# Issuing the value loads of an attention + token-mixer kernel on Scalar's DMA queue instead of Sync's

## Chip, cores, metric

One core of one Trainium2 chip. The metric is the device time of one execution in microseconds (us), the median of several runs. "Fast" runs alone are compared; a run is called slow when it is over 1.5% above the fastest of the same kernel. PE is the matmul engine, PEld its weight load, DVE Vector, ACT Scalar, POOL GpSimd, SP Sync. ACTq and SPq are the instruction sequencers of ACT and SP, which also issue the DMAs (140 of 141 on SP, one on ACT in the trace of before).

## The reference

Eight batches, each with 8 heads, 576 positions and 64 channels: local attention (a band of 7 keys) plus attention over groups of four positions, then a token mixer with w_q, w_k and w_out.

```python
q_d, k_d, v_d = (mean of 4 neighbours of q, k, v)            # 144 positions
out_up    = np.repeat(sm_attn(q_d, k_d, v_d), 4, axis=2)
mask      = np.abs(pos[:, None] - pos[None, :]) < 4
out_local = softmax(where(mask, scale * q @ k.T, -1e9)) @ v
x = (out_up + out_local)                                      # (8, 576, 512)
W = (x @ w_q) @ (x @ w_k).T / sqrt(64)
return np.maximum(W @ x, 0) @ w_out                           # 8 x 576 x 512, float32
```

## The kernel before

In this kernel every DMA is issued by one engine, in its program order (Sync's timeline shows the ten v loads of a batch one behind the other, 10.27 us). The value loads are ten per batch, one for each half of five windows: 64 partitions x 8 heads x 64 channels, 128 KB in pieces of 256 bytes.

```python
def load_qk(b):      # q and k 1 MB each, then the remainders r (two loads of 128 KB), all on sp
    ...
def load_v(b):
    v32 = st[b]["v32"] = big.tile([128, NW, H, D], FP32, name="v32", tag="v32")
    for n in range(NW):                       # NW = 5
        for c in range(2):
            sp.dma_start(v32[64 * c:64 * c + 64, n],
                         _ap(v[b], K0[2 * n + c] * D, [[D, 64], [S * D, H], [1, D]]))
...
load_qk(0); load_v(0)                         # then w_q, w_k, load_qk(1), w_out; load_v(1) falls
...                                           #   between "tq" and "tk" of batch 0 (order below)
ORDER = [                                     # one period; (lag, step)
    (-2, "og1"), (-1, "wtd"), (0, "sums"), (1, "cast_qk"), (-1, "wt"), (0, "vd"), (0, "mask0"),
    (0, "score0"), (-1, "wks"), (2, "load_qk"), (1, "cast_v"), ...
    (0, "cs0"), (-1, "mx1"), (0, "cs1"), (0, "av4"), (0, "weights"), (-1, "mxr"), (1, "tq"), (0, "ca0"),
    (2, "load_v"), (-1, "og0"), (0, "ca1"), (1, "tk"), (1, "tr"), (-1, "ol"), (0, "xt0"), (0, "xt1"),
    (0, "odt"),
]
```

What matters of ACT's work: `tq` and `tk` end in its copies qT and kT (PSUM to SBUF), `og0` and `og1` in its copies os, `odt` in odT. `load_v(2)` stands in the order right behind qT and ahead of the first os. Other names in the profiles: PE writes the PSUM tiles pq and pk (transposes of q and k, copied to qT and kT), psc and pav (scores, and their product with v), pcs (scores of the groups), px and pod (transposes, copied to xT and odT), pwd (which needs odT) and po (the output, copied to os). E and Ec are the exponentials of the scores; kd and kdt are sums of four keys.

The softmax here doesn't subtract the row's maximum and nothing guards it: scores larger than these inputs give would overflow.

Of the kernel before, what the change touches and what calls it, by code (L numbers as in the profile page):

```python
# [13 lines left out]
def _ap(t, off, dims):  # L14

    return bass.AP(t.tensor, t.offset + off, dims)
# [14 lines left out]
def kernel(  # L31
# [12 lines left out]
    sp = _InOrder(tc, nc.sync)  # L44
    pool = _InOrder(tc, nc.gpsimd)
    act = _InOrder(tc, nc.scalar)
# [54 lines left out]
    def load_v(b):  # L101
        v32 = st[b]["v32"] = big.tile([128, NW, H, D], FP32, name="v32", tag="v32")
        for n in range(NW):
            for c in range(2):
                sp.dma_start(v32[64 * c:64 * c + 64, n],
                                  _ap(v[b], K0[2 * n + c] * D, [[D, 64], [S * D, H], [1, D]]))

    st = [{} for _ in range(B)]
    load_qk(0)
    load_v(0)  # L110
    wqk16 = cst.tile([128, 4, 2 * DH], FP16, name="wqk16")
    wo16 = cst.tile([128, 4, DM], FP16, name="wo16")
# [488 lines left out]
    for b in range(B):  # L601
        d_ = {"load_qk": (lambda b=b: load_qk(b)), "load_v": (lambda b=b: load_v(b)),
              "weights": weights if b == 0 else (lambda: None)}
        for stage in (stage_cast, stage_a, stage_b, stage_c):
            d_.update(stage(b))
        steps.append(d_)
# [36 lines left out]
```

## Time and profile before

| | before |
|---|---|
| median of 3 runs | 193.03 us (192.62 to 193.21) |
| steady period per batch | 19.30 us |
| kT of batch 0 starts | 16.32 us |
| vblk of batch 0 (first tile that gates the attention) | 27.20 us |

From the page of the kernel before: busy time by engine, the DMA queues (packets, MB, share of 16 engines), and the chain that ended last, by engine.

```profile
PE 155.5 (81%) x2720; PEld 104.0 (54%) x2720; DVE 114.8 (60%) x286; ACT 110.7 (57%) x140; POOL 107.7 (56%) x122
...
q1 hardware_dynamic: 73920, 40.12, 81.7%
...
PE 68%; DVE 17%; ACT 7%; issue 4%; POOL 2%; ACTq 0%; DVEq 0%
```

PE is the longest in the sum and carries two thirds of the chain. Nearly all data goes through one queue, q1, which is Sync's.

### The profile page before, as it was taken

The numbers are of one execution on the slowest core, as the hardware profiler recorded it, in microseconds if no ns is written. First come the engines' busy times: TensorE is split into PE (matmuls) and PEld (weight loads), VectorE is DVE, ScalarE is ACT, GpSimd is POOL, SyncE is SP. The second block draws the span as 40 slices with busy tenths as digits, with TensorE's granted clock in tenths as the row PEclk, the third lists the DMA queues.
The fourth block names the chain that finished last, engine by engine and source line by source line (L and its number), as shares of the span: only waits on it lengthen the run. The fifth ranks groups of instructions, "written<-read, shape, count | busy, mean of one in ns | idle before, by whom it ended". The sixth has DMA issues, their size and how long they took to land.

```text
span 192.7 us, 6374 instructions
## 1 busy us (share of the span) xinstructions
PE 155.5 (81%) x2720; PEld 104.0 (54%) x2720; DVE 114.8 (60%) x286; ACT 110.7 (57%) x140; POOL 107.7 (56%) x122
## 2 busy tenths in 40 slices
PE   0034448885899989998999899989998999898790
PEld 0034227853576647664776476647764776465330
DVE  6263978754646566656665666566656665685220
ACT  2037134954565767576757675767576757633422
POOL 5701991099748991895479547954895476000000
PEclk9999555999789999999999999999999999999997
DMA  5999999899899799967999899969996943004215
GB/s 175 314 187 215 348 290 162 191 354 175 175 319 218 174 264 294 263 137 201 278 323 156 184 280 346 187 154 296 330 215 154 300 146 112 3 3 153 93 57 188
DMA packets 74027, 40.54 MB, mean 210 GB/s; under 512 B 52432, under 2 KB 68880, under 8 KB 74000
## 3 DMA queue, kind: packets, MB, share of 16 engines
q1 hardware_dynamic: 73920, 40.12, 81.7%
q8 instruction: 21, 0.34, 0.7%
q14 instruction: 6, 0.05, 0.1%
q10 hardware_dynamic: 80, 0.03, 0.1%
HBM read 30.67 MB, written 9.44 MB: 208 GB/s over the span
## 4 chain that ended last, share of the span: by engine, by line
PE 68%; DVE 17%; ACT 7%; issue 4%; POOL 2%; ACTq 0%; DVEq 0%
PE po L27 15%; PE psc L27 6%; PE pav L27 5%; PE pw L27 4%; PE px L27 4%; PE pca L27 4%; PE pol L27 4%; DVE kd_127 L27 3%; PE pv L27 2%; PE pcs L27 2%; ACT kT L27 2%; PE pod L27 2%; DVE rz L27 1%; PE pws L27 1%; PE pwd L27 1%
## 5 line engine op out<-in xcount | busy, mean ns | idle before, releaser
L27 ACT COPY os<-po 128x1024 f32<-128x1024 f32 x16 | 16.2, 1012 | 14.7 <-issue 8.3
L27 DVE RECIPROCAL rz<-pav 128x8 f32<-128x8 f32 x40 | 8.1, 204 | 13.4 <-PE pav L27 13.4
L27 PE MATMUL po<-wo_91,rmx_227 128*128 128x512 f16 x64 | 15.3, 379 | 0.6 <-ACT rmx_227 L27 0.6
L27 PE MATMUL po<-wo_91,rmx_212 128*128 128x512 f16 x64 | 15.1, 379 | 0.0
L27 DVE COPY xT<-px 128x928 f16<-128x928 f16 (+1 forms) x32 | 13.8, 451 | 0.6
L27 PE MATMUL pq_236<-id_67,q_229 128*128 128x128 f16 x16 | 1.9, 312 | 12.6 <-DVE q_229 L27 12.6
L27 PE MATMUL psc<-id_67,neg 64*128 64x232 f16 (+1 forms) x80 | 9.4, 278 | 2.8 <-DVE vblk_201 L27 2.8
L27 PEld LDWEIGHTS <-rmx_227 128*128 128x128 f16 x80 | 7.2, 98 | 8.1 <-ACT rmx_227 L27 0.7
L27 PE MATMUL psc<-qT,kT 64*64 64x58 f16 (+1 forms) x640 | 11.4, 198 | 0.0
L27 PEld LDWEIGHTS <-rmx_212 128*128 128x128 f16 x80 | 7.2, 98 | 6.6
L27 DVE RECIPROCAL rc<-pca 128x8 f32<-128x8 f32 (+1 forms) x16 | 3.4, 211 | 11.8 <-PE pca L27 11.8
L27 PEld LDWEIGHTS <-wqk_90 128*128 128x128 f16 x96 | 8.3, 98 | 3.7 <-issue 0.9
L27 PEld LDWEIGHTS <-kT 64*64 64x64 f16 x640 | 8.7, 113 | 2.1 <-issue 2.1
L27 ACT COPY odT<-pod 128x448 f16<-128x448 f16 (+1 forms) x16 | 5.6, 402 | 6.3 <-PE pod L27 6.3
L27 PE MATMUL pw<-xT,wqk_90 128*128 128x288 f16 x64 | 9.2, 286 | 0.0
L27 PEld LDWEIGHTS <-q_229 128*128 128x128 f16 x16 | 1.6, 146 | 12.6 <-DVE q_229 L27 12.6
L27 POOL CAST v_0_147<-v_79 128x2560 f16<-128x2560 f32 x1 | 3.1, 3129 | 9.3 <-DMA w_92<-in_moe_w_k_dram 9.3
L27 DVE TENSOR_TENSOR wT_219<-pw,wTd 128x576 f16<-128x576 f32 x4 | 3.0, 758 | 8.6 <-ACT wTd L27 8.6
L27 DVE COPY ol<-pol 64x512 f32<-64x512 f32 x8 | 5.5, 682 | 4.3 <-PE pol L27 4.3
L27 DVE TENSOR_TENSOR wT_204<-pw,wTd 128x576 f16<-128x576 f32 x4 | 3.0, 758 | 8.0 <-ACT wTd L27 6.6
L27 DVE TENSOR_SCALAR rmx_227<-pmx 128x1024 f16<-128x1024 f32 x4 | 4.9, 1224 | 4.1 <-PE pmx L27 4.1
L27 POOL CAST v_1_149<-v_255 128x2560 f16<-128x2560 f32 x1 | 2.3, 2323 | 8.6 <-DMA v_255<-in_v_dram 8.6
(542 smaller groups left out, 540.9 us busy)
## 6 DMA issues: line engine op xcount, KB each, us to landing
out_dram<-os SPq DMA_DIRECT2D x16, 512.0 KB, 4.4
v_79<-in_v_dram SPq DMA_DIRECT2D x10, 128.0 KB, 4.6
v_255<-in_v_dram SPq DMA_DIRECT2D x10, 128.0 KB, 5.4
v_583<-in_v_dram SPq DMA_DIRECT2D x10, 128.0 KB, 3.5
v_1024<-in_v_dram SPq DMA_DIRECT2D x10, 128.0 KB, 4.4
v_1497<-in_v_dram SPq DMA_DIRECT2D x10, 128.0 KB, 3.6
v_1970<-in_v_dram SPq DMA_DIRECT2D x10, 128.0 KB, 4.3
v_2443<-in_v_dram SPq DMA_DIRECT2D x10, 128.0 KB, 3.4
```

The costliest lines, as they stand in the source:

```text
L27: return lambda *a, **k: self._tc.keep_in_program_order(f_(*a, **k))
```

## The change

The intent: Sync issues almost without a pause, Scalar is busy 57% of the time, so let Scalar's queue take the loads of v.

```diff
         for n in range(NW):
             for c in range(2):
-                sp.dma_start(v32[64 * c:64 * c + 64, n],
+                act.dma_start(v32[64 * c:64 * c + 64, n],
                                   _ap(v[b], K0[2 * n + c] * D, [[D, 64], [S * D, H], [1, D]]))
```

## The prediction

> **What bounds the kernel now.** I read the page's busy shares first, then three periods of the steady loop as windows, then the Sync and Scalar engines' own timelines, and last the chain of work that ended last. The windows each run from one copy of kT to the next:
>
> ```profile
> core 0: us, PE busy (x) PEld busy (x) DVE busy (x) ACT busy (x) POOL busy (x), PEclk, DMA share, GB/s
> 96.59:115.90 19.31, 18.53 (x344) 12.44 (x342) 12.33 (x30) 13.23 (x18) 13.59 (x12) 1.00 0.93 235
> 135.19:154.49 19.30, 18.52 (x344) 12.43 (x342) 12.31 (x30) 13.22 (x17) 13.59 (x12) 1.00 0.91 246
> ```
>
> PE is busy 18.5 of 19.3 us in each batch's period: the steady loop is PE's. DMA is at 0.93, so close behind, and ACT has 6.1 us of room. Who issues what is in the timeline of the Sync engine's queue (start, duration, tile), one period of it:
>
> ```profile
> 91.00 0.46 SPq L27 DMA_DIRECT2D q_1710<-in_q_dram  x1
> 91.56 1.80 SPq L27 DMA_DIRECT2D k_1711<-in_k_dram  x1
> 93.44 3.63 SPq L27 DMA_DIRECT2D r_1712<-in_q_dram  x1
> 97.13 1.40 SPq L27 DMA_DIRECT2D r_1712<-in_k_dram  x1
> 98.62 10.27 SPq L27 DMA_DIRECT2D v_1970<-in_v_dram  x10
> 108.99 1.13 SPq L27 DMA_DIRECT2D out_dram<-os  x1
> 110.21 0.51 SPq L27 DMA_DIRECT2D out_dram<-ol  x1
> 110.81 0.72 SPq L27 DMA_DIRECT2D out_dram<-os  x1
> ```
>
> Sync issues without a pause for about 20 of each 20 us, half of it for the ten v loads. That looks like a bound, but the period stays 19.30 us in the stretch where the last loads run out, so Sync is just keeping up and nobody waits for it in the loop. One v load by itself (tile view; min/median/max in ns):
>
> ```profile
> L27 SPq DMA_DIRECT2D v_1497<-in_v_dram x10: 633/976/2201, 77.0 to 88.2; - x10
> ```
>
> The minimum, 633 ns (with 45 ns to the next: 0.68 us), is the bare issue; the larger values come at the head of a block, right behind q and k (2 MB). Now the place in Scalar's work where the block will go, between qT and the first os:
>
> ```profile
> 111.33 0.38 ACT L27 ACTIVATE rmx_227<-pmr 128x256 f16<-128x256 f32 x1 [0.18 <-PE pmr L27]
> 112.34 1.86 ACT L27 COPY qT<-pq_2408 128x2048 f16<-128x2048 f16 x1 [0.63 <-PE pq_2408 L27]
> 114.53 1.01 ACT L27 COPY os<-po 128x1024 f32<-128x1024 f32 x1 [0.32 <-PE po L27]
> 115.90 1.86 ACT L27 COPY kT<-pk_2480 128x2048 f16<-128x2048 f16 x1 [0.36 <-PE pk_2480 L27]
> 118.49 0.70 ACT L27 COPY odT<-pod 128x448 f16<-128x448 f16 x2 [0.73 <-PE pod L27]
> 120.26 1.01 ACT L27 COPY os<-po 128x1024 f32<-128x1024 f32 x1 [1.07 <-issue]
> ```
>
> Between qT's end (114.21) and os there are 0.3 us, not ten issues' worth. In the start-up the chain runs through the very copy that the second block of loads will stand in front of:
>
> ```profile
> 14.55 1.86 ACT qT L27
> 16.42 1.78 ACT kT L27
> 18.22 1.37 DVE sum_296 L27
> 19.61 5.71 DVE kd_127 L27 x4
> 25.32 1.88 DVE kdt_129 L27
> 27.20 0.68 DVE vblk_201 L27 x2
> 27.93 0.37 PE psc L27 x2
> ```
>
> [...]a v load holds Sync 0.63 us and lands 3.6 us after its start (median). [...]a wait record of ACT starts at 112.37, while qT (112.34 to 114.21) is still copying. But another wait record stands directly ahead of qT, at 112.29: it waits for PE's transposes, and the sequencer passes it only when qT can start. [...]the trace has such a window (clock 0.5 from 50.6 to 54.0) after PE's idle gap of 46.2 to 48.5.
>
> **The change part by part.** Nothing is removed or added; PE, DVE and POOL keep their instruction order. Eighty DMA issues leave Sync for Scalar, as eight blocks of ten, each in one piece: v of batch 0 ahead of everything on ACT, v of batch 1 between qT and kT of batch 0, the others after qT of the next batch. Each DMA also waits for one of eight completion counters, that is, for the landing of an earlier DMA, now across both queues.
>
> *Five loop blocks (batches 3 to 7), exposed.* Measure from e, the end of the second os copy (101.97 in the period shown, 121.28 the next: 19.3).
> - Until qT nothing changes: 112.34 - 101.97 = e+10.4.
> - The block starts there (the wait ahead of qT). Sync is now free at e, so q, k and the r pair are issued at once. By the page's packets they need about 8.9 us of the engines with os and 2 us of latency, about e+11.5; the block's waits for their landing (fifth load on) are met. So 10 x 0.68 = 6.8 us: end at e+17.2.
> - os 1.0 (e+18.3), kT 1.86 (e+20.1). PE had run on through ca, po, pk, pol to e+15, then stands: px needs the PSUM tile that os empties, and the next po the one that kT empties. po 1.73: e+21.9, second os 1.0: e+23.0.
> - Period 23.0 against 19.3: +3.7, less than the 4.8 us that os comes later, as odT and its wait overlap kT. Five periods: +18.5.
>
> *Half clock.* PE stands some 3.4 us per period. That may drop its clock in a following window, as it did after the 2.3 us gap. A window at half clock costs up to 1.7; I take 0.8 on average: +4 for five.
>
> *The block of batch 2.* Its qT has one wait only, with no wait record ahead of it, so the sequencer can issue the block while the copies ahead of it still stand in the queue (E4, Ec0, Ec1, two weight casts, qT: several us of waits). Hidden: 0.
>
> *Start-up, two blocks.* The first block competes with q and k[...], and neg, the table load and the cast of k stand behind it in order. The last v load waits for the second r, neg for the w_q load, which waits for a landing too. Estimate from packet times (1 KB 46 ns, 256 B 18 ns, on 16 engines) and 2 us latency: k lands about 11.5 (before 9.8), neg leaves at 14.3, k's cast ends at 18 (before 11.8). The second block waits in turn for q, r and wo of batch 1 and k of batch 2: first load at 19.5, k of batch 2 lands about 32.7, block done at 34, so kT starts at about 34.4 instead of 16.4: +18. The chain shown (DVE sums, vblk, psc) follows whole. It is my least certain term (+10 to +24).
>
> *Sum:* 193 + 18.5 + 4 + 18 = 233; the start-up's PE work is at half clock already and a part of my landing estimates is pessimistic, so I take 230.
>
> **The rivals.**
> - *Room on ACT hides it (same time).* 13.2 busy plus 6.8 of issue is 20.0, less 1.9 that lies under qT: 18.1 of 19.3. By sum it fits. Against it: ACT's room is scattered in gaps of 0.2 to 1.2 us, and the block is in one piece at a place with 0.3.[...]
> - *Two queues are faster (faster by some per cent).* Sync is full, DMA at 0.93, outputs leave 12 us after os is copied (75.9 to 88.9). Against: the loop is PE's at 18.5 of 19.3, and the start-up chain waits for q and k, which now share the DMA engines with v. At best v of batch 0 comes earlier, and the 5 us of PE wait for it at 16.7 to 21.8 go: 188. I hold this unlikely.
> - *Back-pressure makes the block longer.* If ACT's issues are held as Sync's first v loads are (1.2 to 2.2 us, 10 to 11.8 a block), a period becomes 26 to 27: +35 to 40 in the loop, 245 to 255. Against: in the new order q and k have drained when the block starts.
>
> **Range and chances.** Loop +12 (partly hidden) to +30 (back-pressure, half clock), start-up +10 to +24: 214 to 247 holds it 8 times in 10. Slower by over 2% 0.96, within 2% 0.03, faster 0.01.
>
> **What would show it.** Right: the v blocks on ACTq start with qT and take about 6.8 us each; os follows each block at once, with ACT idle for about 5 us before it; period near 23 us from batch 3's block on, and back to 19.3 after the last; PE waits at px for os; kT of batch 0 starts near 34; DMA share falls below 0.85. Wrong: blocks that start well ahead of qT (sequencer runs ahead), blocks of 10 us (back-pressure), kT of batch 0 before 25, or a period under 20.5.

Parts of the recorded texts, here and below, are cut (each cut is marked). No term of the sum is cut: 193 + 18.5 + 4 + 18 was put as 233 and taken as 230. Gone are the argument that moving issues wins no bandwidth, and a depth to which Scalar's sequencer can run ahead, with the 205 to 215 us of the first rival that rested on it. What stays is shown in the trace of the kernel before as follows:

- Completion counters: the 141 DMAs use eight semaphores. In all 101 cases in which the trace has the landing of the DMA that had the semaphore last, the next one on it starts after that landing.
- Packet times: medians of 46 ns for 1 KB and 18 ns for 256 B. The "2 us latency": the shortest time from issue to landing is 2.28 us (ol, 128 KB), of which 64 packets of 2 KB at 86 ns on 16 engines are some 0.34.
- Half clock: the granted clock was 0.5 for 3.41 us (50.62 to 54.03), and half of that is the 1.7 of the text. The average of 0.8 is the author's guess.
- A sequencer ahead of its engine: by one wait record (112.37, within qT's 112.34 to 114.21). That it gets ahead of the copies named in batch 2 was the author's guess.
- That the first block competes with q and k: shown only afterwards, by k of batch 0, which landed at 12.46 us with the block in place and at 9.85 before.

## The result, and the profile after

The changed kernel takes **236.36 us** (median of 4 runs, 234.43 to 238.32) against 192.94 (4 runs, one more than in the table above, 192.62 to 193.21): slower, ratio 1.222, 95% interval 1.2141 to 1.2298. Here and below a ratio is the mean time of one kernel's fast runs over that of the other's of the same rounds, so not quite the ratio of the medians quoted. The profiled run is a fast one with a span of 235.7 us, against 192.7 before: 43.0 us more.

The same lines of the page as above, of the changed kernel:

```profile
PE 160.6 (68%) x2720; PEld 105.1 (45%) x2720; DVE 109.1 (46%) x286; ACT 109.3 (46%) x140; POOL 106.8 (45%) x122
...
q1 hardware_dynamic: 31680, 29.63, 44.4%
...
q10 hardware_dynamic: 42320, 10.52, 22.0%
...
PE 45%; DMA 20%; ACT 12%; DVE 9%; ACTq 7%; issue 5%; SPq 0%; DVEq 0%
```

The busy times hardly change, so no work was added. The chain did: DMA, ACT and ACT's sequencer now carry 39% of it. (Issuing is not counted as busy, so ACT's 46% hides the blocks of loads.)

**The loop.** Two periods of the changed kernel as windows, from one second os to the next (length, then busy time and count of PE, PEld, DVE, ACT and POOL, clock, DMA share, GB/s):

```profile
90.57:113.49 22.92, 19.07 (x340) 12.37 (x340) 12.41 (x29) 12.96 (x19) 13.58 (x13) 1.00 0.79 213
113.49:135.92 22.43, 19.03 (x340) 12.43 (x340) 12.40 (x29) 12.94 (x18) 13.58 (x13) 1.00 0.80 218
```

22.4 to 22.9 us instead of 19.3, with PE standing for 3.4 to 3.9 us (length less PE's busy time) and the DMA engines less loaded (0.79 against 0.93). Scalar's own timeline shows the cause (start, duration, instruction; in brackets how long ACT idled and who ended it):

```profile
103.33 1.87 ACT L27 COPY qT<-pq 128x2048 f16<-128x2048 f16 x1 [0.87 <-PE pq L27]
103.41 6.79 ACTq L27 DMA_DIRECT2D v<-in_v_dram  x10
110.24 1.01 ACT L27 COPY os<-po 128x1024 f32<-128x1024 f32 x1 [5.04 <-PE px L27]
```

The block begins 0.08 us after qT and holds the sequencer for 6.79 us; os follows 0.04 us after it. PE's po, which os empties, was finished at 105.43 (103.54 + 1.89). The bracket names PE's px because its semaphore was the last the profile saw; the sequencer was in fact at the loads. In the kernel before, the same os stood 0.3 us after qT.

**The start-up.** ACT's timeline of the first two blocks, and behind it the chain of waits of the changed kernel:

```profile
0.80 15.02 ACTq L27 DMA_DIRECT2D v<-in_v_dram  x10
...
22.02 22.00 ACTq L27 DMA_DIRECT2D v<-in_v_dram  x10
44.06 1.87 ACT L27 COPY kT<-pk 128x2048 f16<-128x2048 f16 x1 [20.72 <-DMA v<-in_v_dram]
```

```profile
1.31 11.15 DMA k<-in_k_dram
12.48 5.18 DMA v<-in_v_dram
...
18.33 10.09 DMA r<-in_k_dram
28.49 14.22 DMA k<-in_k_dram
...
44.06 1.88 ACT kT L27
...
47.36 0.85 DVE kd L27 x4
```

The second block takes 22 us where ten bare issues take 6.8. Six of its loads start 0.02 to 0.03 us after the landing of an earlier DMA: three of Sync's, and three v loads of Scalar's own. Four of the six:

| load of the second block starts | a landing just before |
|---|---|
| 22.02 | q of batch 1, 22.00 |
| 27.01 | last v of batch 0 (Scalar's own), 26.98 |
| 30.70 | w_out (first half), 30.68 |
| 42.73 | k of batch 2, 42.71 |

The kernel has eight completion counters for its DMAs: in the trace its 141 DMAs use eight semaphores, 17 or 18 each. Each of the 133 DMAs that follow another on its semaphore starts after that one's landing, 20 of them 0.02 to 0.05 us after it (on either queue, behind landings of either queue). So here a DMA that takes a counter waits until the DMA that took it last, eight places earlier in the order in which they are handed out, has landed, whichever engine issued it. That is not the order of the source: k of batch 2 comes in it ahead of the ninth v load of batch 1. On Sync alone the wait was nearly free: in the kernel before, each v load of a block starts 0.04 to 0.05 us after the end of the issue ahead of it, and none of the 101 DMAs for which that trace has the landing on their counter starts within 0.06 us of it. Split over two queues, Scalar at batch 0 waits for k of batch 2.

**Where the 43.0 us came from.** From the times of the same instructions in both traces:

| | before | after | added |
|---|---|---|---|
| start-up: vblk of batch 0 | 27.20 | 48.39 | +21.2 |
| block of batch 2: kT of batch 1 | 37.05 | 62.91 | +25.9, so +4.7 more |
| block of batch 3: second os of that period | 62.37 | 90.57 | +28.2, so +2.3 more |
| four more blocks: periods of 22.92, 22.43, 23.70, 22.50 | 19.30 each | | +14.4 |
| the last periods | | | +0.4 |

In the start-up kT comes 27.7 us later, but some 6.5 us are given back: the four DVE sums kd took 5.71 us before and 0.85 now, and kdt 1.88 and 0.18. POOL was at work beside them before and is idle now. In the trace of before three of the four sums end 0.14 us after the POOL instruction beside them (21.89 after 21.75, 23.99 after 23.85, 25.32 after 25.18); the fourth, which started just ahead of its POOL instruction, took 0.27. That POOL's work held them is the author's reading of these times: no experiment moved it away. The third row mixes causes: before has a PE gap and half clock between 46.19 and 54.0 in it, after has half clock from 63.7 to 70.5. The period of 23.70 also holds a PE gap of 1.18 us of the kind that experiments 9 to 11 are about.

### The profile page after: what moved, and what is told of

It is laid out like the page before. It is cut to its first block, busy times and chain, and to the rows that moved or that the text cites. A ratio compares the mean times of both kernels' runs of the same rounds, so it can differ in the third digit from the quotient of the medians.

```text
span 235.7 us, 6369 instructions
## 1 busy us (share of the span) xinstructions
PE 160.6 (68%) x2720; PEld 105.1 (45%) x2720; DVE 109.1 (46%) x286; ACT 109.3 (46%) x140; POOL 106.8 (45%) x122
## 4 chain that ended last, share of the span: by engine, by line
PE 45%; DMA 20%; ACT 12%; DVE 9%; ACTq 7%; issue 5%; SPq 0%; DVEq 0%
DMA k<-in_k_dram 11%; ACTq L27 7%; PE po L27 7%; PE pm L27 6%; DMA v<-in_v_dram 5%; ACT kT L27 5%; PE psc L27 5%; DMA r<-in_k_dram 4%; DVE x L27 4%; PE pav L27 4%; PE pw L27 4%; ACT Ec L27 3%; PE pq L27 3%; PE pcs L27 2%; PE pol L27 2%
## 5 line engine op out<-in xcount | busy, mean ns | idle before, releaser
L27 POOL TENSOR_TENSOR sum<-qT 128x1152 f32<-128x1152 f16 x8 | 16.9, 2107 | 45.0 <-DVE qT L27 45.0
L27 POOL CAST v<-v 128x2560 f16<-128x2560 f32 x8 | 18.6, 2326 | 33.8 <-DMA r<-in_q_dram 17.7
L27 PE MATMUL po<-wo,rmx 128*128 128x512 f16 x128 | 30.5, 380 | 3.6 <-DVE xT L27 3.0
L27 DVE TENSOR_TENSOR x<-pav,rz 128x512 f16<-128x512 f32 x40 | 27.7, 692 | 1.4
L27 ACT COPY kT<-pk 128x2048 f16<-128x2048 f16 x8 | 15.0, 1870 | 26.1 <-DMA v<-in_v_dram 25.8
L27 PEld LDWEIGHTS <-rmx 128*128 128x128 f16 x160 | 14.2, 98 | 18.5 <-DVE xT L27 3.8
L27 POOL TENSOR_TENSOR sum<-kT 128x1152 f32<-128x1152 f16 x7 | 14.8, 2107 | 15.3 <-ACT kT L27 15.3
L27 ACT ACTIVATE E<-psc 128x928 f16<-128x928 f32 (+1 forms) x24 | 19.5, 812 | 3.7 <-PE psc L27 2.7
L27 PE MATMUL pav<-v,E 64*64 64x65 f16 x640 | 18.3, 199 | 3.8 <-issue 1.2
L27 PEld LDWEIGHTS <-E 64*64 64x64 f16 x640 | 14.9, 113 | 11.9 <-issue 8.6
L27 PE MATMUL pq<-id,q 128*128 128x128 f16 x128 | 10.1, 242 | 12.9 <-DVE q L27 12.7
L27 ACT COPY qT<-pq 128x2048 f16<-128x2048 f16 x8 | 14.9, 1865 | 4.3 <-PE pq L27 4.3
```

The costliest lines, as they stand in the source:

```text
L27: return lambda *a, **k: self._tc.keep_in_program_order(f_(*a, **k))
```

## The experiments

All twelve kernels were correct.

### 1. The loop's blocks alone

```diff
-                act.dma_start(v32[...
+                (act if b >= 2 else sp).dma_start(v32[...
```

> The loads of values of batches 0 and 1 are back on Sync; batches 2 to 7 stay on Scalar in their blocks of ten. Theory (a block holds Scalar between qT and the copy after it): start-up as before (kT of batch 0 at 16.3 us), about +3.6 us in each of five loop periods and +5 us for batch 2: 193 + 22 = 215 us, 211 to 219. Rival (nearly all of the loss is the start-up, the loop only has a slightly longer period through shared DMA engines): at most 203 us.

Measured: 227.38 us (225.53 to 229.18) against 193.96, ratio 1.1674 (1.1584 to 1.1764). More than the 211 to 219 expected, so a miss, and more than the loop's share in the whole change. The start-up is that of before (kT at 16.31). The block of batch 2 took 1.37 + 10.16 us: its fifth to ninth load each start 0.02 us after the landing of the block's own load four places earlier (37.18 after 37.16, for example), as Sync's DMAs had taken the other four counters, and those own loads took 3.0 to 6.5 us to land. So kT of batch 1 came 8.7 us later. The following periods were 24.7, 22.8, 27.0 and 22.8 us. The blocks in them (6.8 to 7.9 us) are those of the whole change; the two longer ones also hold a stretch of half clock, behind a 1.67 us wait of PE for Ec in the first and behind a PE gap of 2.99 us with no releaser, only "issue", in the second. So the blocks explain about 22.8 a period, and something else the rest: experiments 9 to 11.

### 2. The first block alone

```diff
+                (act if b == 0 else sp).dma_start(v32[...
```

> Only the ten loads of batch 0 on Scalar. Theory (the block stands ahead of neg, the table load and the cast of k): k's cast starts about 10 us later than before (9.9), kT about 7 us later (near 23), part of which comes back as the DVE sums no longer run beside POOL: 196 to 201 us. Rival (the first block is free because Scalar waits for k anyway, the second block is the whole start-up loss): 192 to 194 us.

Measured: 201.86 us median of 199.24, 204.49, 198.57 and 204.91, two of them slow runs, so no interval; the fast two, 198.57 and 199.24, are some 5 us above before and agree with the expectation (profiled span 197.2). kT of batch 0 starts at 22.96 (16.32 before), as the cast of k stands behind the ten issues in ACT's order, and vblk at 32.19.

### 3. The second block alone

```diff
+                (act if b == 1 else sp).dma_start(v32[...
```

> Only the ten loads of batch 1 on Scalar, between qT and kT of batch 0. Theory (the block waits for landings of Sync's q, k, r and wo loads through the shared counters, beyond its bare 6.8 us): the block takes 12 to 22 us, kT of batch 0 starts at 27 to 37 instead of 16.3, and the time is 200 to 212 us. Rival (only the bare issue counts): block 6.8 us, kT at about 22, 193 to 198 us.

Measured: 195.99 us, ratio 1.0099 (1.0041 to 1.0157): below the range, a miss. The block took 10.85 us and kT came 9.1 us later, but vblk only 4.1 us later:

```profile
28.74 2.42 DVE L27 TENSOR_TENSOR kd<-sum 128x116 f16<-128x116 f32 x4
```

2.42 us for the four sums where before has 5.71. Of a delay ahead of those sums a part is returned by them. Of the 4.1 us some 2 more were made up later, as the median is 2.0 above that of before. The trace has no PE gap by "issue" (experiments 9 to 11) and from 38.1 us on no half clock, where before has both; whether this made them up was not tested. All four waits of the block, once begun, were for its own earlier loads, not for Sync's q, k, r and w_out as the expectation had it.

### 4. All of v in the start-up (batches 0 and 1)

```diff
+                (act if b < 2 else sp).dma_start(v32[...
```

> Batches 0 and 1 on Scalar, batches 2 to 7 on Sync: the start-up of the changed kernel alone. Theory (the two blocks feed each other: the first holds back Sync's loads of batch 1 through the counters, and the second waits for exactly those): kT of batch 0 near 44 us and vblk near 48 us as in the changed kernel, 193 + 21 = 214 us, 210 to 218, although the blocks alone cost about 6 and 2. Rival (the two just add up): 199 to 204 us.

Measured: 213.98 us, ratio 1.0976 (1.091 to 1.1043): as expected. The second block takes 21.38 us and kT of batch 0 starts at 42.66. One block costs 5 us (fast runs), the other 2, both 20: the second waits for landings that come later with the first in place (k of batch 2 at 40.63; the load that waits for it starts at 40.65). The costs of the parts do not add up, and the waits for landings, of both queues, are why.

### 5. The loads spread over ACT's period

Batches 0 and 1 on Sync; the ten loads of the others on ACT, one or two at a time behind E0, E1, E4, mx0, qT, os and kT.

```diff
-        (0, "score0"), (-1, "wks"), ...
+        (0, "score0"), (2, "lv0"), (-1, "wks"), ...        # lv0 .. lv9: one load each, on act
```

> Batches 0 and 1 on Sync; the ten loads of batches 2 to 7 stay on Scalar, but one or two at a time behind long copies (E, rmx, qT, os, kT), where the sequencer issues while the engine copies. Theory (the place of the block is what costs, not the queue): the period goes back to 19.3 to 20.0 us and the time to 192 to 197 us. Rival (Scalar's issue time or the sharing of DMA engines between two queues costs by itself, wherever it stands): 6.8 us more of Scalar's time per batch, 205 to 217 us.

Measured: 221.73 us (215.74 to 225.43, three of the four runs slow): a clear miss. A load by itself still takes 0.60 at best, but others last up to 1.92, and others again start only behind a landing of q, k or r, in whose flight they are issued (a load at 107.92 behind q's landing at 107.90; one at 114.31 behind k's at 114.29). The profiled run has a mean clock of 0.873.

### 6. The same, only where q, k and r have landed

Loads behind qT (2), os (1), kT (2), odT (1), the second os (1), E0 (1), E1 (2); POOL's cast of v moved behind the last of them.

> As the first spread version, but the ten loads stand where q, k and r of the period have already landed: two behind qT, one behind os, two behind kT, one behind odT, and in the next period one behind the second os and three behind the E copies. Theory (the first spread version failed because its loads waited on Scalar for landings of q, k and r through the shared counters, and PE's clock fell for it): no load waits more than 0.3 us, the period is 19.3 to 20.3 us and the time 193 to 201 us. Rival (loads on Scalar cost their issue time wherever they stand, or sharing the DMA engines slows the loop): 208 us and more.

Measured: 210.57 us, ratio 1.0828 (1.0748 to 1.0909). The expectation failed as a time, but one of its periods came out as hoped. Windows of this run, from second os to second os:

```profile
93.04:112.93 19.89, 18.77 (x344) 12.39 (x341) 12.33 (x29) 13.20 (x17) 11.47 (x11) 1.00 1.00 248
112.93:136.03 23.10, 20.10 (x344) 12.93 (x342) 12.42 (x29) 13.30 (x18) 15.67 (x15) 0.93 0.83 213
```

19.89 us holds all ten issues on ACT with only 0.6 us lost: there is room for them in pieces. The next period has a PE gap of 2.44 us by "issue" and a clock of 0.93.

### 7. Twenty half loads a block

```diff
+                for h2 in range(2):                        # 32 partitions each, batches 2 to 7
+                    act.dma_start(v32[64 * c + 32 * h2:64 * c + 32 * h2 + 32, n], ...
```

> As the version with only the loop's blocks on Scalar (227 us), but each load is cut in two of 32 partitions, so 20 issues of half the descriptors per block. Theory[...]: an issue takes near 0.35 us, a block stays at 7 to 8.5 us and the time at 222 to 236 us. Rival (a fixed cost per issue): 0.65 us each, a block of 13 us and more, six blocks of 6 us: 255 us and more.

Measured: 261.69 us, ratio 1.3471. ACT's timeline, the block of one period:

```profile
105.19 10.99 ACTq L27 DMA_DIRECT2D v<-in_v_dram  x20
```

The same bytes, but 10.99 us instead of 6.79. A half load holds the sequencer 0.46 us with 0.50 from one to the next, a whole one 0.65 with 0.69. By these two points an issue costs about 0.31 us (estimated: 2 x 0.50 - 0.69) plus 0.38 for its 512 pieces. The block's length sets the time in this direction: with twenty issues the period of this block is 27.9 us (from 91.56 to 119.47, at a clock of 0.93, so part of it is half clock). The block of batch 2 took 23.61 us, with landings in its way again.

### 8. The start-up's sums in one instruction (kernel before otherwise)

```diff
+                if b == 0:
+                    add(kd.rearrange(...)[:, :, :, 0:29], s_[..., 0], s_[..., 1], op=ALU.add)   # all 4 pairs
```

> The kernel before with one change elsewhere: the four sums kd of batch 0 on DVE are one instruction. In the kernel before each of these small DVE instructions ends only when a POOL instruction beside it ends (5.7 us for four), in the changed kernel, with POOL idle, the four take 0.85 us. Theory (each DVE instruction waits out one POOL instruction, so fewer instructions wait less): kd and kdt end 3 to 5 us earlier and the time is 188 to 191 us. Rival (the slowdown goes by the amount of work, or the chain has another end): 192 to 194 us.

Measured: 193.77 us against 194.01, ratio 1.0004 (0.9939 to 1.0068): no gain. (Of the four sums of before, it is three that end with a POOL instruction, 0.14 us after it.) The sum took 2.64 us in one piece, the four 5.71 before, and vblk came 2.9 us earlier (24.26), so the sums' own delay shrank as thought, but the time was lost again further on; the trace shows two PE gaps by "issue" (30.10 to 31.21 and 45.90 to 47.29) that were open at that point.

### 9 to 11. What is the PE gap by "issue"?

Every such gap of a microsecond or more, in all these runs (12 in the runs without filler), stands at 193 or 194 of PE's instructions modulo 256; in the two looked at closest (before and experiment 1) it is in the middle of a row of equal matmuls of one tile. The trace's PE instructions, counted in order of start, and the packets of the DMA queue named "instruction" (21 of 16 KB in the kernel before); five of the gaps:

| kernel | PE stands | ahead of PE instruction no. | modulo 256 | last packet | PE goes on after the packet's end |
|---|---|---|---|---|---|
| before | 46.19 to 48.52 | 961 | 193 | 45.64 to 46.99 | 1.53 |
| after | 142.76 to 143.93 | 3010 | 194 | 141.57 to 142.56 | 1.37 |
| experiment 1 | 129.34 to 132.34 | 3010 | 194 | 129.90 to 130.84 | 1.50 |
| experiment 6 | 77.95 to 79.89 | 1729 | 193 | 77.43 to 78.60 | 1.29 |
| experiment 6 | 119.30 to 121.74 | 3010 | 194 | 119.27 to 120.26 | 1.48 |

The gaps stand whole multiples of 256 instructions apart (give or take one), and 21 packets against 5440 PE instructions (2720 matmuls, 2720 weight loads) make 259 to a packet. The author's reading is that these packets bring PE's instructions, 256 in each, and that a gap is a late packet. To test it, 64 one-column matmuls (128 PE instructions with their weight loads) went in where PE waits for v in the start-up anyway. That moves every later multiple of 256 by 128 instructions against the work.

```diff
             v16, vd0, vblk = g["v16"], vd0S[b % 2], vblkS[b % 2]
+            if b == 0:
+                pad = psm(name="pad")
+                for i in range(64):
+                    pe.matmul(pad[:, i:i + 1], id16, id16[:, i:i + 1], start=True, stop=True)
             pv = ps(name="pv")
```

In the kernel before:

> Question: what are the gaps of PE that the profile puts down to "issue" (before: 46.19 to 48.52, ahead of pav, followed by a clock of 0.5 from 50.6 to 54.0)? In all runs so far they stand at PE instruction number 449, 961, 1729 or 3010 of the trace, all 193 or 194 modulo 256, and in each a 16 KB packet of the queue 'instruction'[...] is in flight. Theory: PE stands because the next 256 instructions come late. Edit: the kernel before with 64 matmuls of one column (128 PE instructions with their weight loads) put where PE waits for v anyway (16.6 to 21.8). The theory says: no such gap ahead of the matmul that was number 961; if there are any, they stand at 193 modulo 256 of the new count (65 of the old). Time: if no new gap takes its place, 193.9 less 2.3 and less the 1.7 of the half clock: 189 to 191; if one does, 193 to 195. Rival: the gap belongs to that matmul's place (a wait the profile does not show): it stays ahead of the same matmul, and the time stays within 1 us or rises by what the filler costs.

In the kernel of experiment 1:

> The loop's blocks alone on Scalar (227.4, with 'issue' gaps of 1.85 and 2.99 us at numbers 961 and 3010) with the same 128 filler instructions. Theory (late instructions): no gap ahead of those two matmuls; 227.4 less 4.8 of gaps and less about 3 of half clock: 218 to 222 if no others appear, up to 228 if others do at numbers 193 modulo 256 of the new count. Rival (place): the gaps stay, 226 to 230.

In the kernel of experiment 6:

> The late spread (210.6, with 'issue' gaps of 1.94 and 2.44 us and half clock behind each) with the same filler. Theory: gaps move to numbers 193 modulo 256 of the new count or vanish; if they vanish, periods near 19.9 throughout and 198 to 204; if they move to other places where PE is not waiting, 208 to 212. Rival (place): gaps stay ahead of pcs and pav, 210 to 213.

Measured: 193.21 us against 193.41, ratio 0.9973 (0.9912 to 1.0035); 224.56, ratio 1.1549 (1.1438 to 1.1661); 208.37, ratio 1.0684 (1.0578 to 1.079). First the place of the gap, PE's timeline of the kernel before, then of the same matmuls in experiment 9:

```profile
45.97 0.23 PE L27 MATMUL pav<-v_1_149,E_1_143 64*64 64x65 f16 x3
48.52 0.38 PE L27 MATMUL pav<-v_1_149,E_1_143 64*64 64x65 f16 x13 [2.33 <-issue]
```

```profile
46.98 0.43 PE L27 MATMUL pav<-v,E 64*64 64x65 f16 x16
```

Before, 3 of 16 matmuls run and the other 13 come 2.33 us later; with the filler all 16 run in one piece. In experiment 9 no gap by "issue" of 0.9 us or more is left, and the half clock of 50.6 to 54.0 is gone. Experiments 10 and 11 lost their old gaps (at 961 and 3010, at 1729 and 3010) and each has one new one, both ahead of instruction 2497 of the new count: 193 modulo 256 again, a place that had no gap before (2369 of the old count, 65 modulo 256). PE goes on 1.43 and 1.48 us after the end of the packet. So the gap belongs to a place in the count of PE's instructions, not to the work: shown. That PE waits there for the packet is the author's reading of the 1.29 to 1.53 us from a packet's end to PE's going on. Why a gap comes at a given place in one run and not in another stays open.

What a gap costs when it comes, from two windows of experiment 10, from second os to second os:

```profile
97.80:125.53 27.73, 21.29 (x340) 13.89 (x340) 12.41 (x29) 13.02 (x18) 13.56 (x13) 0.88 0.67 177
125.53:148.32 22.79, 19.13 (x340) 12.44 (x340) 12.41 (x29) 12.95 (x19) 13.57 (x13) 1.00 0.79 215
```

The first has the gap (2.80 us) and half clock from 107.5 to 114.3: 4.9 us more than its neighbour. This fits the longest period of experiment 1 (27.0): without a gap the period is 22.5 to 22.8, that of the whole change. Its period of 24.7 has half clock behind another wait, and why PE lost its clock there and not behind similar waits of the whole change is open. In experiment 11 the periods without a gap are 19.9, the one with it 23.7.

The times hardly followed, though: 193.21 is not resolved from 193.41, where the expectation had 189 to 191 without a gap, a miss. Experiments 10 and 11 have medians 2.8 and 2.2 us below those of 1 and 6 (other chips, other rounds, and the intervals of the ratios overlap), each having traded two gaps for one. The first second os of the loop came 2.2 us earlier in experiment 9 than before, and its profiled span was 191.0 against 192.7; but runs of the kernel before vary by as much, perhaps because its gap is not in every run, which only a profile of each could show.

### 12. Half of each block on ACT

```diff
+                (act if b >= 2 and c else sp).dma_start(v32[...
```

> Of the ten loads of batches 2 to 7, five (the second half of each window) go to Scalar, five stay on Sync; batches 0 and 1 stay on Sync. Question: is the price proportional to the block's length, or is there room that takes a short block? Theory (room of about 3 us: the whole block made os 6.8 - 1.9 = 4.8 us later and the period 3.6 longer): five bare issues end 3.4 us after qT's start, 1.6 after its end, os is 1.5 later, and the period is 19.3 to 19.9 except where a landing wait or a late instruction fetch falls: 194 to 200. Proportional rival: half of what the blocks of the loop cost in the whole change (5.0 + 2.3 + 14.4 = 22 us), 203 to 206. Third possibility (loads wait for the landings of loads on the other queue, as in the loop alone, 227): blocks of over 6 us for five loads, over 206.

Measured: 215.65 us (213.26 to 218.52), ratio 1.1008 (1.0922 to 1.1094): the theory fell, the third possibility held. ACT's timeline:

```profile
104.69 6.44 ACTq L27 DMA_DIRECT2D v<-in_v_dram  x5
111.25 1.01 ACT L27 COPY os<-po 128x1024 f32<-128x1024 f32 x1 [4.85 <-DMA v<-in_v_dram]
```

Five loads hold ACT for 6.44 us, almost as long as ten did; the others of the run took 3.57 (batch 2), 5.55, 7.65, 6.03 and 4.14. Two loads are issued at once; the third starts at 108.14 behind the landing of k at 108.12, the fourth at 109.24 behind r's at 109.22, the fifth at 110.52 behind that of the block's own first load at 110.50. In the whole change k (issued at 92.65) took 10.9 us and landed at 103.57, just as the block started (103.41). Here, with v loads on Sync right behind q, k and r, k (issued at 95.26) took 12.9 us and landed 3.4 us after the block's start: the waits fall into the block. That the v loads of Sync are what slows k is argued, not shown. The price of loads on ACT is not their count alone; the landings that its loads wait for, of the other queue and of their own, set it too.

## Why the prediction was right, and in which terms it was not

The size (230 predicted, 236 measured, inside 214 to 247) and the main mechanism held. Term by term:

- **Loop blocks, +18.5 for five: right in kind, 1.8 too high.** Blocks of 6.79 to 8.03 us where 6.8 was predicted, starting with qT, os right behind, ACT idle 5.04 us ahead of it, DMA share 0.79. The blocks of batches 3 to 7 added 2.3 + 14.4 = 16.7. Period 22.4 to 23.7 against 23.0. The 16.7 include 1.18 of a PE gap by "issue". Within the period two errors cancel: qT starts 10.8 to 11.7 us after e in the four periods, not 10.4, as PE still waits for odT at the head of the period (0.49 to 1.73); and behind the block there is less than the step assumed, for PE does not stop at px. The trace has px at 107.72, before os, and its second half at 109.51 after 1.07 us: with two of three PSUM tiles waiting for ACT, PE goes on with the third.
- **Half clock, +4: wrong, 0.** No half clock in the four loop periods. (The one stretch of it, 63.7 to 70.5, comes with a wait of PE for odT of 4.59 us behind the block of batch 2.) PE's standing comes in pieces (1.07 at px, 0.60 at po, up to 1.73 at pwd), not in the one piece of 3.4 that the step assumed. The 2.3 us gap that it was modelled on was another thing, tied to the count of PE's instructions (experiments 9 to 11). The length of a gap does not settle it: behind the 2.33 us of before and the 1.67 of experiment 1 came half clock, behind 1.73 and 1.18 us in the changed kernel none; what tells them apart was not shown. Where such a gap falls into the loop, as in experiment 10, it costs 4.9.
- **Block of batch 2, hidden, 0: wrong, +4.7.** The step that failed is that a copy with one wait, and no wait record ahead of it, lets the sequencer pass. The block began at 56.05, with qT at 55.99. What held it was qT's own wait for PE's transposes pq, the last of which ended at 55.95: the first record of the sequencer behind qT, a wait, is at 55.99. Experiment 1 tells this from a sequencer that cannot be ahead of its engine. There pq ended at 33.86, and two loads left ahead of qT, which stands before them in the program:

```profile
32.81 1.05 PE L27 MATMUL pq<-id,q 128*128 128x128 f16 x16
34.14 1.37 ACTq L27 DMA_DIRECT2D v<-in_v_dram  x2
35.06 1.88 ACT L27 COPY qT<-pq 128x2048 f16<-128x2048 f16 x1
```

Here the first record behind qT is at 33.91, when not even the weight cast ahead of qT (34.12) had begun. In the seven traces with such a record behind this qT (the changed kernel, experiments 1, 6, 7, 10, 11 and 12) it comes 0.04 to 0.05 us after the end of pq. So in these traces this copy held what is behind it until its own wait was met, and no longer.

- **Start-up, +18: right in mechanism, mis-sized, +21.2.** kT of batch 0 was put at 34.4 and started at 44.06: the landing that it hangs on, k of batch 2, was estimated at 32.7 and came at 42.71. It was late from the start: the cast of k ended at 21.58, not 18. Against that, 6.5 us came back in the DVE sums, which the step did not have. Experiment 4 shows the two blocks as one chain (20 us, where each alone costs 5 and 2).
- **The sum.** 233 was cut to 230; the trace gives 21.2 + 4.7 + 2.3 + 14.4 + 0.4 = 43.0, 6 more than the 37 predicted. Two terms were missing (+4.7 in batch 2, -6.5 in the sums), one was superfluous (+4), one too small (start-up landings). That the total is only 6 off is in part luck: the superfluous +4 nearly makes up for the missing +4.7, and the sums for most of what the landings were late.

The rivals: *room on ACT* is refuted for a block in one piece (22.4 to 22.9 us), yet the room exists for single loads (19.89 in a period of experiment 6). *Two queues are faster* is refuted: no run that has v on ACT beat the kernel before. *Back-pressure* as written (10 to 11.8 us a block) did not occur in the whole change's loop, where only one issue of ten in three of the five blocks was longer (1.07 to 1.88 us); but its kin, waiting for landings, made the blocks of 22 us in the start-up and of 10 to 14 us for batch 2 in experiments 1 and 10.

No version here beats the kernel before; the filler and the merged sum equal it.

## What to carry to other kernels

In this kernel an issue of a DMA took its place in the order of the engine that issues it: ten in a row at 0.68 us were a 6.8 us hole, however idle the engine was on average (57% busy), so ask what stands right behind them and who waits for that. The eight completion counters coupled the two queues: in the block of 22.00 us six of the ten loads started 0.02 to 0.03 us after a landing, three of them of the other queue and three of Scalar's own, and with Sync's DMAs on the other four counters a load waited for its own block's load four places earlier (experiment 1). So check which DMA had the counter last (here eight places earlier) and when it lands before splitting. And read a PE gap by "issue" at its place in the instruction stream (here 193 or 194 modulo 256) before putting it down to data.
